# Banded attention and a gated projection on one core: two rotating pairs of score banks, a joint maximum, convolution from SBUF, and a new written order

## The chip, the cores and the metric

The kernel runs on one core of one Trainium2 chip. Its engines work from queues of their own, each in order: TensorE (PE, whose weight loads are shown apart as PEld), VectorE (DVE), ScalarE (ACT), GpSimd (POOL), and SyncE (SP), which here issues DMA transfers. PSUM, where PE writes, has eight banks of 512 float32 columns for each of 128 partitions; the DVE and ACT instructions of this kernel read it, its POOL instructions do not. The metric is the device time of one execution in microseconds (us), lower is better.

## The reference

Two stages follow one another. The first is attention with a window of 128 keys and 4 sink keys, for 4 batches, 8 heads, 768 positions and 64 columns a head:

```python
scores = scale * np.matmul(q, k.transpose(0, 1, 3, 2))
keep = is_sink | in_window          # key < 4, or 0 <= query - key < 128
scores = np.where(keep, scores, -1000000000.0)
scores = scores - np.max(scores, axis=-1, keepdims=True)
a = np.exp(scores)
a = a / (np.sum(a, axis=-1, keepdims=True) + 1e-09)
return np.matmul(a, v).astype(np.float32)
```

The second takes the heads side by side as x (768 x 512 a batch), gates a projection of x with a causal convolution of five taps, and projects again:

```python
for k in range(K):
    gate_pre += conv_w[k][None, None, :] * xp[:, k:k + S, :]
gate = 1.0 / (1.0 + np.exp(-gate_pre))
val = x @ w_val
return (gate * val @ w_out).astype(np.float32)
```

## The kernel before, in words

**Tiling.** The work is cut into 24 steps s, each a batch b, one of three blocks of 256 queries p (so p is s // 2 % 3), and one of two groups of four heads. Two steps that follow one another (the two groups of heads) make one of 12 tiles m of the second stage. In step s:

- load_kq (kq) and load_v (vv) fetch keys, queries and values; the tiles of keys and of queries have three buffers each.
- scores(s, g) for g = 0 and 1 (s0, s1) issues 32 small matmuls into the two banks ss (L364), patches the band with a predicated copy (L369), and takes in four instructions the masked, negated scores to SBUF and their extremes to ngm (L374).
- exps (e0, e1) computes four exponentials with their sums on ACT (L382). recip (rec, L387 and L388) inverts the sums on DVE. normalise (norm, L396 to L403) scales on POOL.
- probs_t (tx, ty) transposes on PE (L413), each half into one of two banks tr. probs_x (ev) masks on DVE (L435, L437), probs_y (yv) copies on ACT (L444). sinks_t and sinks_e (sk, ts) do the same for the sink columns.
- values and sinks (val, si) multiply by the values on PE into the two banks xv (L461, L468). x_copy and x_high (xc, xh) copy the result out on ACT (L478, L482); x_low (xl) makes the remainder on POOL (L492). x_head (hd) writes the last four columns of the block before in front of xv, in PSUM.
- conv_last (c4, POOL, L496) makes the last tap; conv (c0, c1, L504) adds the other four on DVE, eight instructions a step, reading x from PSUM and the running sum from SBUF. gate (th, L509) is a tanh on ACT.

For each tile m: val (v0 to v3, L523) is the first projection in four blocks of 12 matmuls, gated (g0, g1, L534) multiplies on DVE from PSUM, gated_h and gated_l (h, l; L538, L542) split into high and low parts on ACT and POOL, outp (o0 to o3, L553) is the second projection in blocks of 6 matmuls, store (t0, t1, L557) copies out and stores. Both projections, the sink transposes and the weight decoding share two banks acc. Banks: ss 2, xv 2, tr 2, acc 2.

**Start.** The weights come as 64-bit floats and are decoded on ACT, DVE, POOL and PE (load_weights, decode_weights; events l and a to f of each of four chunks of w_val and w_out) between the first steps. Matmuls of zeros (busy, L225) stand before and between the first scores.

**Order.** Nothing is planned while building: every event has a due time, its step plus a number of the tables WHEN and EARLY (or DECODE), the events are sorted by it, and each engine's queue is filled in that order:

```python
for _, f, args in sorted(events, key=lambda e: e[0]):
    f(*args)
```

Of the kernel before, what the change touches and what calls it, by code (L numbers as in the profile page):

```python
# [35 lines left out]
WHEN = dict(kq=-1.9615, vv=-0.3611, s0=-0.1928, e0=0.4814, s1=0.3255, e1=0.5848, rec=0.6245, vl=1.4302, norm=0.667,  # L36
            tx=0.9562, ty=1.2383, sk=1.1919, ev=1.1901, yv=1.3942, ts=1.226, val=1.8427, si=1.874, xc=2.044,
            xh=2.2668, hd=2.0069, xl=2.2917, c4=2.0938, c0=2.2838, c1=2.5363, th=2.774, v0=0.4208, v1=0.4433,
            v2=0.7542, g0=0.6699, v3=0.8679, h0=0.7252, l0=1.0416, g1=0.9504, h1=1.0551, l1=1.282, o0=1.3729,
            o1=1.5265, o2=1.3969, t0=2.127, o3=2.081, t1=2.5321, cw=-67.148)  # L40

EARLY = {("kq", 0): -111.3041, ("vv", 0): -51.6322, ("s0", 0): -67.4875, ("e0", 0): -63.9472, ("s1", 0): -63.8218,
# [156 lines left out]
def banded(ctx, tc, wts, cw, zero, ident, scalars, flag, qt, kt, vt, vsk, w_val, conv_w, w_out, out):  # L199
# [393 lines left out]
    for t in skb:  # L593
        nc.gpsimd.memset(t, 0.0)
# [211 lines left out]
```

## Time and profile before

| what | value |
|---|---|
| three runs | 282.65, 279.63, 282.4 us; median 282.4 |
| span of the profiled execution | 279.6 us (no time outside the span is listed) |
| PE busy | 264.6 us (95%) |
| DVE busy | 221.2 us (79%) |
| ACT busy | 181.0 us (65%) |
| POOL busy | 175.4 us (63%) |
| granted PE clock, mean | 0.987 |

A line of the groups reads: line, engine, operation, tile written <- tiles read, shape, count | busy us, mean ns of one | idle us of the engine before them, and what ended it. The chain of waits is followed back from the last instruction to whatever released each one; its pieces are shown in order of time. Busy PE time is modelled from pipelined matmuls, so it is not PE at its peak.

### The profile page before, as it was taken

To read this page: it belongs to the slowest core of one execution; us is meant where nothing else is said; L and a number is where in the kernel's file an instruction comes from. 1 tells how busy PE (TensorE), PEld (TensorE's weight loads), DVE (VectorE), ACT (ScalarE), POOL (GpSimd) and SP (SyncE) were. 2 spreads that over 40 slices of the span, in tenths; PEclk is the share of its full clock that TensorE was granted. 3 is DMA by queue.
4 is the path that set the end of the run, shared out by engine and by line. 5 is a ranking of instruction groups with operands and counts; after the bars stand their busy time and mean duration, and the time that the engine had idled before them with its cause. 6 is when DMAs were issued, how large, how long until landed. Compare 5 with 4: busy or idle time off the path is not lost.

```text
span 279.6 us, 9649 instructions
## 1 busy us (share of the span) xinstructions
PE 264.6 (95%) x3748; PEld 211.1 (75%) x3752; DVE 221.2 (79%) x827; ACT 181.0 (65%) x605; POOL 175.4 (63%) x226
## 2 busy tenths in 40 slices
PE   8897599999999999999999999999999999999991
PEld 3444358769878879789789788788788788798880
DVE  5899969997879787986977987996896898887510
ACT  3799949838757765764875784685676667564421
POOL 3378956883965874675585757648658729647330
PEclk9999989999999999999999999999999999999997
DMA  6993952028416515516417317326336241020202
GB/s 191 328 373 129 303 158 96 4 85 291 140 49 212 157 38 194 155 41 211 140 40 246 101 67 225 101 84 205 97 93 212 87 134 56 6 75 0 77 5 82
DMA packets 27396, 36.95 MB, mean 132 GB/s; under 512 B 2256, under 2 KB 23760, under 8 KB 27344
## 3 DMA queue, kind: packets, MB, share of 16 engines
q1 hardware_dynamic: 27344, 36.27, 40.4%
q8 instruction: 31, 0.51, 0.8%
q14 instruction: 21, 0.17, 0.2%
HBM read 29.97 MB, written 6.29 MB: 130 GB/s over the span
## 4 chain that ended last, share of the span: by engine, by line
PE 77%; POOL 7%; DVE 7%; ACT 5%; issue 1%; POOLq 0%; ACTq 0%
PE acc L523 23%; PE acc L553 21%; PE xv L461 11%; PE ss L364 9%; PE tr L413 5%; PE acc L225 3%; PE xv L468 3%; POOL wx L396 2%; DVE sg L504 2%; ACT w L382 2%; DVE sx L374 2%; POOL sg L496 1%; ACT xt L478 1%; POOL xl L492 1%; POOL wol L179 1%
## 5 line engine op out<-in xcount | busy, mean ns | idle before, releaser
L396 POOL TENSOR_TENSOR wx<-w,sm 128x512 f32<-128x512 f32 x48 | 49.2, 1047 | 59.9 <-DVE sm L388 53.2
L504 DVE SCALAR_TENSOR_TENSOR sg<-xv,cw,sg 128x256 f32<-128x256 f32 x192 | 78.9, 475 | 5.9 <-POOL sg L496 5.9
L382 ACT ACTIVATE w<-sx,ngm 128x132 f32<-128x132 f32 x192 | 75.1, 399 | 4.1 <-DVE ngm L374 4.1
L523 PE MATMUL acc<-xh,wvh 128*128 128x256 f32 x192 | 49.3, 291 | 0.4 <-ACT xh L482 0.4
L523 PE MATMUL acc<-xh,wvl 128*128 128x256 f32 x192 | 47.1, 279 | 0.0
L374 DVE CUSTOM_DVE_ANT_0 sx<-ss,mask 128x132 f32<-128x132 f32 x192 | 45.2, 292 | 1.6
L553 PE MATMUL acc<-woh,gh 128*128 128x512 f32 x96 | 40.0, 416 | 0.0
L364 PE MATMUL ss<-k,q 64*32 64x168 f32 x1536 | 38.5, 309 | 1.4 <-DVE ngm L374 0.8
L523 PEld LDWEIGHTS acc<-xh,wvh 128*128 128x128 f32 x192 | 36.1, 188 | 3.8 <-DVE sg L504 1.3
L553 PE MATMUL acc<-wol,gh 128*128 128x512 f32 x96 | 38.1, 397 | 0.3 <-POOL wol L179 0.3
L553 PE MATMUL acc<-woh,gl 128*128 128x512 f32 x96 | 38.1, 396 | 0.0
L382 ACT ACTIVATION_READ_ACCUMULATOR w<-sx,ngm 128x1 f32 x192 | 37.2, 194 | 0.0
L461 PEld LDWEIGHTS xv<-wt,v 64*64 64x64 f32 x1024 | 30.3, 133 | 8.1 <-issue 5.1
L523 PEld LDWEIGHTS acc<-xh,wvl 128*128 128x128 f32 x192 | 36.1, 188 | 0.0
L542 POOL TENSOR_TENSOR gl<-sg,gh 128x512 fp32r<-128x512 f32 x24 | 31.5, 1312 | 5.7 <-ACT gh L538 5.7
L461 PE MATMUL xv<-wt,v 64*64 64x192 f32 (+2 forms) x1024 | 34.5, 278 | 0.5 <-ACT wt L444 0.5
L496 POOL TENSOR_TENSOR sg<-xt,cw 128x512 f32<-128x512 f32 x24 | 25.2, 1051 | 11.4 <-ACT xt L478 11.3
L364 PEld LDWEIGHTS ss<-k,q 64*32 64x32 f32 x1536 | 22.4, 106 | 12.8 <-issue 3.6
L492 POOL TENSOR_TENSOR xl<-xt,xh 128x512 fp32r<-128x512 f32 x24 | 30.9, 1289 | 1.7 <-ACT xh L482 1.7
L523 PE MATMUL acc<-xl,wvh 128*128 128x256 f32 x192 | 30.9, 281 | 0.9 <-POOL xl L492 0.9
L413 PE MATMUL tr<-ident,wx 128*128 128x128 f32 x192 | 28.2, 274 | 0.0
L523 PEld LDWEIGHTS acc<-xl,wvh 128*128 128x128 f32 x192 | 26.0, 188 | 1.4 <-POOL xl L492 1.3
(110 smaller groups left out, 423.5 us busy)
## 6 DMA issues: line engine op xcount, KB each, us to landing
k<-in_kt_dram SPq DMA_DIRECT2D x23, 408.0 KB, 4.0
v<-in_vt_dram SPq DMA_DIRECT2D x16, 384.0 KB, 3.3
out_dram<-osb SPq DMA_DIRECT2D x24, 256.0 KB, 2.1
q<-in_qt_dram SPq DMA_DIRECT2D x23, 256.0 KB, 4.3
raw<-in_w_val_dram SPq DMA_DIRECT2D x4, 512.0 KB, 6.7
v<-in_vt_dram SPq DMA_DIRECT2D x8, 256.0 KB, 4.2
raw<-in_w_out_dram SPq DMA_DIRECT2D x4, 512.0 KB, 6.2
vs<-in_vsk_dram SPq DMA_DIRECT2D x8, 128.0 KB, 4.1
```

The lines of the kernel that those rows point to most:

```text
L364: nc.tensor.matmul(ss[e * QB:(e + 1) * QB, j, c * n + x0:c * n + x1], q[js, g, (4 * c + e) * QB:(4 * c + e + 1) * QB], k[js, g, (2 * c + e ...
L374: nc.vector.tensor_tensor_reduce(out=sx[:, j, c], in0=sv[:, j, c, :PK], in1=mask[:, c if p == 0 else 2], op0=ALU.add, op1=ALU.min, scale=- ...
L382: nc.scalar.activation(out=w[:, g, j, c], in_=sx[:, j, c], func=AF.Exp, scale=-1.0, bias=ngm[:, g, j, c:c + 1], accum_out=sm[:, g, j, c:c ...
L396: nc.gpsimd.tensor_tensor(out=t[:, n].rearrange("p c h x -> p h c x"), in0=w[:, :, :, at], in1=sm.to_broadcast([P, 4, 2, D]), op=ALU.mult)
L413: nc.tensor.transpose(out=x[:, o:o + P], identity=ident, in_=ws[s][:, n, c, 2 * g:2 * g + 2].rearrange("p j x -> p (j x)"))
L461: nc.tensor.matmul(acc[o * D:(o + 1) * D, g, x0 + h * D:x0 + (h + a1 - a0 + 1) * D], v[js, g, n], t[js, g, n, a0:a1 + 1].rearrange("p a r ...
L492: nc.gpsimd.tensor_tensor(out=xl[:, g], in0=xts[s], in1=xh[:, g].bitcast(F32), op=ALU.subtract)
L496: nc.gpsimd.tensor_tensor(out=sg[s // 2][:, g], in0=xts[s], op=ALU.mult, in1=cw[:, g, KT - 1:].to_broadcast([P, 2, PQ]))
L504: nc.vector.scalar_tensor_tensor(out=g, in0=x, scalar=a, in1=g, op0=ALU.mult, op1=ALU.add)
L523: nc.tensor.matmul(acc[:, h], a[:, kc, cs], x[:, kc], start=(n == 0), stop=(n == 11))
L542: nc.gpsimd.tensor_tensor(out=gl, in0=g, in1=gh.bitcast(F32), op=ALU.subtract)
L553: nc.tensor.matmul(acc, a[:, kc, ts], x[:, kc], start=(kc + n == 0), stop=(kc + n == 5))
```

## The change

- **Banks.** ss and tr go. Two pairs of banks take their place, handed out in turn by pair() to each scores call and each probs_t call (tx, which now does both halves), in the order of the list. Banks: pairs 4, xv 2, acc 2.
- **Maximum.** In steps with p above 0 the four instructions of L374 are replaced by one maximum over the four blocks, straight from PSUM, and a small scaling by -0.125; the exponentials then read the pair of banks in PSUM with scale 0.125. Steps with p = 0 keep the four instructions with the mask.
- **Convolution.** x_copy writes x to SBUF behind four columns for the head, x_head copies the head there too, and conv reads SBUF (six buffers xt in place of four).
- **First projections.** val_copy (y0, y1) copies a projection out to SBUF on ACT; the list has it for m = 0 and 1 only.
- **Start.** The first queries and the first chunk of w_val are fetched over ACT's queue; identity, blanks and the table load (warm_up, now near the end) become events; the index patterns of masks get a place each; the fills of zeros are other counts.
- **Order.** The tables of due times are replaced by one written list. Names are as above, with px, py for ev, yv, sv for the sink values and vl for val(s).

```diff
-    ss = ps_s.tile([P, 2, 512], F32, name="ss", tag="ss")
-    for j in range(2):
-        nc.tensor.matmul(ss[:, j], zero[:, :P], zero, start=True, stop=True)
+    pairs = [ps_s.tile([P, 2, 512], F32, name=f"pr{n}") for n in range(2)]
+    for x in pairs:
+        for j in range(2):
+            nc.tensor.matmul(x[:, j], zero[:, :P], zero, start=True, stop=True)
+
+    def pair():
+        pairs.append(pairs.pop(0))
+        return pairs[-1]
...
+            (nc.scalar if s == 0 else nc.sync).dma_start(out=q[:, hs], in_=qt[b, gs, :, p * PQ:(p + 1) * PQ].rearrange("g p x -> p g x"))
...
+        (nc.scalar if (n, c) == ("wv", 0) else nc.sync).dma_start(out=raw, in_=src)
...
     def scores(s, g):
...
         n = 2 * HB + D
+        ss = pair()
...
+        if p:
+            sxs[s, g] = sv
+            nc.vector.tensor_reduce(out=ngm[:, g], in_=sv[:, :, :, :PK], axis=mybir.AxisListType.X, op=ALU.max)
+            nc.vector.tensor_scalar(out=ngm[:, g], in0=ngm[:, g], scalar1=-0.125, scalar2=None, op0=ALU.mult)
+            return
...
     def exps(s, g):
...
-                nc.scalar.activation(out=w[:, g, j, c], in_=sx[:, j, c], func=AF.Exp, scale=-1.0,
+                nc.scalar.activation(out=w[:, g, j, c], in_=sx[:, j, c, :PK], func=AF.Exp,
+                                     scale=0.125 if steps[s][1] else -1.0,
                                      bias=ngm[:, g, j, c:c + 1], accum_out=sm[:, g, j, c:c + 1])
...
-    def probs_t(s, n):
-        trs[s, n] = x = ps_t.tile([P, 512], F32, name="tr", tag="tr")
...
+    def probs_t(s):
+        trs[s] = x = pair()
+        for n in range(2):
+            for g in range(2):
+                for c in range(2):
+                    o = (2 * g + c) * P
+                    nc.tensor.transpose(out=x[:, n, o:o + P], identity=ident,
+                                        in_=ws[s][:, n, c, 2 * g:2 * g + 2].rearrange("p j x -> p (j x)"))
...
+            xts[s] = p2.tile([P, 2, KT - 1 + PQ], F32, name="xt", tag="xt", bufs=6)
...
     def x_copy(s):
...
+        nc.scalar.activation(out=xt(s)[:, :, KT - 1:], in_=accs[s], func=AF.Copy)
...
-        nc.scalar.activation(out=accs[s][:, :, :KT - 1], func=AF.Copy,
-                             in_=xts[s - 2][:, :, PQ - KT + 1:] if steps[s][1] else none)
+        nc.scalar.activation(out=xt(s)[:, :, :KT - 1], func=AF.Copy,
+                             in_=xts[s - 2][:, :, PQ:] if steps[s][1] else none)
...
-                g, x, a = sg[s // 2][:, c], accs[s][:, h, kk:kk + PQ], cw[:, c, kk:kk + 1]
+                g, x, a = sg[s // 2][:, c], xts[s][:, h, kk:kk + PQ], cw[:, c, kk:kk + 1]
...
+    def val_copy(m, u):
+        t = p2.tile([P, 4, P, 2], I32, name="vc", tag="raw", bufs=4)
+        x = t.rearrange("p k m t -> p (k m t)")[:, :2 * PQ].bitcast(F32).rearrange("p (h r) -> p h r", h=2)
+        nc.scalar.activation(out=x, in_=vacc[m, u], func=AF.Copy)
+        vacc[m, u] = x
...
     with tc.manual_schedule():
-        for _, f, args in sorted(events, key=lambda e: e[0]):
+        for n in ORDER.split():
+            f, args = events[n]
             f(*args)
-            if (f.__name__, args) in FILL:
-                busy(FILL[f.__name__, args])
```

In the list, with all lines left out that the prediction doesn't speak of:

```diff
+ORDER = """
+fill.7 wvl.0 fill.6 fill.4 load_conv kq.0 masks wva.0 wvb.0 hd.0 conv_weights blanks s0.0 fill.6 wvc.0 wvl.2
+wva.2 kq.1 fill.5 vv.0 signs wvd.0 e0.0 wvb.2 wvc.2 s1.0 e1.0 s0.1 e0.1 rec.0 norm.0 wve.0 wvd.2 s1.1 wve.2
...
+s0.2 wvb.1 woe.0 norm.1 wof.0 sk.0 ts.0 tx.1 py.1 px.1 e0.2 wod.0 wva.3 sv.1 wvc.1 rec.2 wvb.3 fill.10 kq.3
...
+woe.3 h1.0 l1.0 tx.3 py.3 wod.3 xh.2 s1.4 e1.4 px.3 rec.4 vv.6 kq.6 s0.6 s0.5 s1.5 o0.0 wof.3 o2.0 o3.0 kq.9
...
+py.5 c4.4 c0.3 c1.3 g0.1 th.3 sk.5 ts.5 sv.6 px.5 g1.1 h0.1 s1.7 l0.1 s1.6 e1.7 h1.1 s0.7 l1.1 vv.7 xl.4 kq.8
+s1.8 e1.6 vl.5 si.5 xh.5 xc.5 o0.1 o2.1 o3.1 vv.9 t1.1 o1.1 t0.1 xl.5 c4.5 v0.2 rec.6 e1.8 norm.6 c0.4 c0.5
...
+ts.6 g1.2 px.7 vl.6 sk.7 si.6 xh.6 xc.6 xl.6 hd.8 c4.6 h1.2 l1.2 ts.7 s1.9 e1.9 kq.11 s0.9 s0.8 vl.7 si.7 xc.7
...
+v3.3 g1.3 tx.9 py.9 px.9 sk.9 ts.9 h1.3 norm.8 tx.8 py.8 px.8 th.6 g0.3 l1.3 h0.3 o0.2 sk.8 ts.8 l0.3 s0.10
+e0.10 hd.13 s1.10 e1.10 kq.12 s0.12 hd.19 s1.11 e1.11 rec.10 norm.10 s0.11 s1.12 e0.11 vl.8 vv.12 o1.2 si.8
+xh.8 xc.8 kq.13 hd.9 vl.9 si.9 o2.3 t0.2 o3.3 xc.9 e0.12 tx.10 xh.9 sk.10 ts.10 vv.10 hd.11 t1.3 e1.12 o0.3
...
+hd.10 h0.4 tx.12 px.12 l0.4 py.12 vl.11 si.11 th.9 xc.11 xh.11 g1.4 vl.12 h1.4 c0.10 vv.13 s0.13 s1.13 s0.14
...
+norm.13 v2.5 v3.5 hd.12 c1.11 e0.14 sv.13 xh.12 xl.12 th.11 g1.5 vv.14 v1.5 g0.5 sk.13 ts.13 tx.13 px.13 kq.16
+s1.14 h0.5 l0.5 py.13 h1.5 e1.14 l1.5 s1.15 vv.16 e1.15 rec.14 c4.12 s0.15 e0.15 s0.16 s1.16 rec.15 vl.13
...
+v3.6 si.14 xh.14 xc.14 c4.14 vv.15 c0.13 c1.13 xl.14 th.12 v1.6 g0.6 vl.15 th.13 g1.6 kq.19 s1.19 h0.6 vv.17
+l0.6 h1.6 e1.19 l1.6 s0.17 e0.17 s0.18 s1.17 tx.16 px.16 si.15 py.16 xc.15 o0.6 o1.6 hd.17 c4.15 c0.15 scalars
...
+h1.7 l1.7 s1.18 kq.20 e1.18 rec.18 s0.19 s0.20 e0.19 vl.17 si.17 xh.17 vv.20 xc.17 o0.7 o2.7 o3.7 c0.16 kq.23
...
+o0.8 norm.20 o1.8 o2.8 vv.22 c4.19 xl.19 c0.18 c1.18 kq.22 o3.8 t1.8 t0.8 tx.20 px.20 sk.20 th.18 py.20 s1.21
+s1.22 e1.21 xl.18 e1.22 ts.20 rec.21 s0.22 e0.22 vl.20 vv.23 v0.9 v1.9 c0.19 si.20 rec.22 xc.20 norm.21 tx.21
...
+s1.23 s0.23 e0.23 si.21 xc.21 e1.23 tx.22 o2.9 o3.9 px.22 py.22 o0.9 hd.22 o1.9 t1.9 xh.21 c0.20 c4.21 xl.21
...
+v3.11 warm_up l0.11 t0.10 g1.11 h1.11 o0.11 o2.11 l1.11 o3.11 t1.11 o1.11 t0.11
+"""
```

More of the change, by code (lines that the diff above doesn't have):

```diff
@@ L34 @@
 BIG = 1.0e30
[L36 to L40, printed above, removed]
@@ L262, in banded @@
     mk = p2.tile([P, 6, P], F32, name="mk", tag="dec_t")
-    d, d0, c4, t0, t1, ti = (mk[:, n] for n in range(6))
+    d, d0, c4, t0, t1 = (mk[:, n] for n in range(5))
     low = cn.tile([P, D], U8, name="low")
@@ L266, in banded @@
     prev = cn.tile([P, D], F32, name="prev")
-    mask = cn.tile([P, 3, PK], F32, name="mask")
+    mask = cn.tile([P, 2, PK], F32, name="mask")
     none = cn.tile([P, 2, KT - 1], F32, name="none")
@@ L306, in banded, with signs, blanks @@
     minus = cn.tile([P, P], F32R, name="minus")
-    nc.gpsimd.tensor_scalar(out=plus, in0=ident, scalar1=1.0, scalar2=None, op0=ALU.mult)
-    nc.gpsimd.tensor_scalar(out=minus, in0=ident, scalar1=-1.0, scalar2=None, op0=ALU.mult)
+    def signs():
+        make_identity(nc, ident)
+        nc.gpsimd.tensor_scalar(out=plus, in0=ident, scalar1=1.0, scalar2=None, op0=ALU.mult)
+        nc.gpsimd.tensor_scalar(out=minus, in0=ident, scalar1=-1.0, scalar2=None, op0=ALU.mult)
     skb = [cn.tile([P, P], F32, name=f"skb{n}") for n in range(2)]
+    def blanks():
+        for t in skb:
+            nc.gpsimd.memset(t, 0.0)
     raws, dec = {}, {}
@@ L406, in banded @@
     probs, trs, skt, sktp = {}, {}, {}, {}
-    def probs_t(s, n):
-        trs[s, n] = x = ps_t.tile([P, 512], F32, name="tr", tag="tr")
-        for g in range(2):
-            for c in range(2):
-                o = (2 * g + c) * P
-                nc.tensor.transpose(out=x[:, o:o + P], identity=ident,
-                                    in_=ws[s][:, n, c, 2 * g:2 * g + 2].rearrange("p j x -> p (j x)"))
+    def probs_t(s):
[6 more added lines that the diff above has]
+                                        in_=ws[s][:, n, c, 2 * g:2 * g + 2].rearrange("p j x -> p (j x)"))
     def sinks_t(s):
@@ L467, in sinks, with xt @@
         for g in range(2):
-            nc.tensor.matmul(accs[s][:, g, KT - 1:KT - 1 + PQ], vs[b, qd][:, g],
+            nc.tensor.matmul(accs[s][:, g], vs[b, qd][:, g],
                              skt[s].rearrange("p c r -> p (c r)"), start=False, stop=True, skip_group_check=True)
     xts = {}
+    def xt(s):
+        if s not in xts:
+            xts[s] = p2.tile([P, 2, KT - 1 + PQ], F32, name="xt", tag="xt", bufs=6)
+        return xts[s]
     def x_copy(s):
-        if steps[s][2] == 0:
-            xs[s // 2] = tuple(p2.tile([P, 4, PQ], F32R, name=n, tag=n) for n in ("xh", "xl"))
-            sg[s // 2] = p2.tile([P, 4, PQ], F32, name="sg", tag="sg")
@@ L477, in x_copy, with half @@
-        xts[s] = t = p2.tile([P, 2, PQ], F32, name="xt", tag="xt", bufs=4)
-        nc.scalar.activation(out=t, in_=accs[s][:, :, KT - 1:KT - 1 + PQ], func=AF.Copy)
+        nc.scalar.activation(out=xt(s)[:, :, KT - 1:], in_=accs[s], func=AF.Copy)
+    def half(d, s, n, dtype):
+        if s // 2 not in d:
+            d[s // 2] = p2.tile([P, 4, PQ], dtype, name=n, tag=n)
+        return d[s // 2][:, 2 * steps[s][2]:2 * steps[s][2] + 2]
     def x_high(s):
-        g, o = slice(2 * steps[s][2], 2 * steps[s][2] + 2), KT - 1
@@ L524, in val @@
             n += 1
+    def val_copy(m, u):
[3 more added lines that the diff above has]
+        vacc[m, u] = x
     def halves(m, u):
         us = slice(2 * u, 2 * u + 2)
+        if m not in gs:
+            gs[m] = tuple(p2.tile([P, 4, PQ], F32R, name=n, tag=n) for n in ("gh", "gl"))
         return sg[m][:, us], gs[m][0][:, us], gs[m][1][:, us]
     def gated(m, u):
[L531 to L532 removed]
         g = halves(m, u)[0]
@@ new lines, in banded @@
+    events = {f"{n}.{x}": (f, (x,) + args) for n, (f, args) in acts.items() for x in range(len(steps))}
+    for f in (masks, signs, blanks, warm_up, scalars, flag, load_conv, conv_weights):
+        events[f.__name__] = f, ()
+    for n in ("wv", "wo"):
+        for c in range(4):
+            events[f"{n}l.{c}"] = load_weights, (n, c)
+            for k in range(6):
+                events[f"{n}{'abcdef'[k]}.{c}"] = decode_weights, (n, c, k)
+    for n in range(1, 20):
+        events[f"fill.{n}"] = busy, (n,)
@@ L728, with warm_up @@
     flag_i = cp.tile([P, 1], I32, name="flag_i")
+    def warm_up():
+        nc.scalar.activation(out=warm, in_=warm, func=AF.Exp)
     def scalars():
```

131 lines of the change are left out of this document (63 added, 68 removed), and 48 rows, old and new, of tables (DECODE, EARLY).

## The prediction

> **What bounds the kernel now.** I read the busy sums by stage first, then the chain of waits in order of time, then the durations by line. The sums by stage (stretch, its length, then busy time and instructions of PE, PE's weight loads, DVE, ACT and POOL, then PE's clock and the DMA):
>
> ```profile
> 0.00:10.00 10.00, 8.59 (x75) 3.45 (x83) 6.63 (x36) 3.50 (x7) 3.85 (x15) 1.00 0.72 215
> 10.00:20.00 10.00, 8.88 (x145) 4.03 (x127) 9.01 (x38) 10.00 (x37) 5.07 (x8) 1.00 1.05 372
> 20.00:30.00 10.00, 7.79 (x94) 5.04 (x94) 9.61 (x31) 9.47 (x29) 9.09 (x13) 1.00 0.57 184
> 30.00:40.00 10.00, 7.73 (x107) 4.34 (x114) 7.71 (x26) 5.91 (x21) 7.43 (x9) 0.83 0.67 226
> 40.00:50.00 10.00, 9.23 (x156) 8.07 (x138) 9.76 (x29) 9.07 (x29) 6.28 (x8) 1.00 0.35 106
> 50.00:60.00 10.00, 9.38 (x109) 6.57 (x102) 9.86 (x36) 6.59 (x25) 8.35 (x8) 1.00 0.01 2
> ...
> 260.00:270.00 10.00, 9.52 (x66) 8.64 (x66) 4.58 (x10) 3.81 (x7) 3.97 (x4) 1.00 0.13 48
> 270.00:279.60 9.60, 3.64 (x16) 2.61 (x14) 0.00 (x0) 1.20 (x2) 0.89 (x1) 0.81 0.18 63
> sum 279.60, PE 264.64 PEld 211.11 DVE 221.24 ACT 181.04 POOL 175.41; mean PE 12.60 PEld 10.05 DVE 10.54 ACT 8.62 POOL 8.35
> ```
>
> Up to 60 us the vector engine is the full one: 6.63 + 9.01 + 9.61 + 7.71 + 9.76 + 9.86 = 52.6 us of 60, so only 7.4 us of it are idle. After that the tensor engine is the full one, as the chain shows. Its columns are start, length, engine, tile and line:
>
> ```profile
> 57.84 2.12 PE acc L553 x8
> ...
> 93.47 0.73 PE ss L364 x32
> 94.20 4.39 PE acc L553 x18
> ...
> 113.53 0.73 PE ss L364 x32
> ...
> 263.34 4.71 PE acc L523 x38
> 268.05 5.60 PE acc L553 x24
> 273.67 0.60 ACT osb L557
> ```
>
> From 93.47 to 113.53 us, one pair of steps, the chain never leaves PE: 20.1 us, with each 0.73 us score group alone between blocks of projections (the 18 at 94.20), values and transposes. So a faster VectorE, ScalarE or GpSimd gains nothing there; only the first 58 us and the tail could give time. From the first output projection at 57.84 to 273.67 PE passes 215.8 us, about 1 us of it idle (0.48 in 260 to 270). Behind it stand 5.9 us of store and DMA.
>
> **The change part by part.** *Score banks.* Today a group of scores has its own pair of banks, free again once VectorE has taken the four maxima. Now scores and transposes take two pairs strictly in turn, and in the 16 steps with p above 0 the exponentials read the pair itself, so it is held until ScalarE is through. The terms, from the timeline (start, duration, engine, line):
>
> ```profile
> 149.95 0.43 DVE L369 COPY_PREDICATED ss<-low,ss 128x256 f32<-128x256 uint8 x1 [0.55 <-PE ss L364]
> 150.41 0.29 DVE L374 CUSTOM_DVE_ANT_0 sx<-ss,mask 128x132 f32<-128x132 f32 x1
> ...
> 151.28 0.08 DVE L374 DVE_READ_ACCUMULATOR2_ANT ngm<- 128x1 f32 x1
> ...
> 155.30 0.41 ACT L382 ACTIVATE w<-sx,ngm 128x132 f32<-128x132 f32 x1
> ...
> 156.77 0.19 ACT L382 ACTIVATION_READ_ACCUMULATOR w<-sx,ngm 128x1 f32 x1
> ```
>
> VectorE's part is 149.95 to 151.36, 1.41 us. Four exponentials last from 155.30 to 156.96, 1.66 us. The single maximum over 4 x 132 values from PSUM and the small scaling are not in the trace. Near rows:
>
> ```profile
> L435 DVE TENSOR_TENSOR wt<-tr,cur 128x512 f32<-128x512 f32 x24 | 16.5, 687 | 9.2 <-PE tr L413 9.2
> L387 DVE TENSOR_SCALAR sm<-sm 128x8 f32<-128x8 f32 x24 | 4.6, 192 | 1.1 <-ACT w L382 1.1
> L478 ACT ACTIVATE xt<-xv 128x512 f32<-128x512 f32 x24 | 14.4, 598 | 9.5 <-PE xv L468 8.8
> L509 ACT ACTIVATE sg<-sg 128x512 f32<-128x512 f32 x24 | 15.0, 625 | 12.0 <-DVE sm L387 7.3 <-DVE sg L504 4.6
> ```
>
> 0.46 + 0.69 + 0.19 = 1.34 us against 1.41: no gain worth counting (bounds 0.2 us either way per group). The exponential from PSUM stays at 1.66 us; the PSUM copy L478 is 4% shorter than L509 from SBUF, and that is its lower bound. So a pair is tied up for 0.73 + 1.41 = 2.14 us with p = 0, and for 0.73 + 1.41 + 1.66 = 3.80 us otherwise, if VectorE and ScalarE are free at once.
>
> *New order.* PE takes the list in order, and the list now puts score groups behind one another with no other PE work between. Behind a waiting group stands all of PE's queue. Walked with the terms above, idle VectorE and ScalarE, and PE's first group at 0:
>
> s0.10, s1.10, s0.12, s1.11, s0.11, s1.12: the third needs the first pair back at 3.80; the fourth waits for e1.10, which ScalarE starts at 3.80, so 5.46; the fifth goes at 6.19; the sixth waits for e1.11 (scores to 6.19, maxima to 7.60, exponentials to 9.26). It ends at 9.99 us for 6 x 0.73 = 4.38 us of work: 5.6 us idle. s1.14, s1.15, s0.15, s0.16, s1.16: starts at 0, 0.73, 3.80, 5.46, 7.60, end 8.33, work 3.65: 4.7 idle. s1.23, s0.23, si.21, tx.22: the transposes need e1.23, which stands behind e0.23 and a 0.60 us copy on ScalarE: 3.55 + 1.66 + 0.60 + 1.66 = 7.47, with 1.7 us done: 5.8 idle. s1.19, s0.17, s0.18, s1.17: 3.3. s1.9, s0.9, s0.8 and s1.21, s1.22, s0.22: third start at 3.80, 2.3 each. s0.13, s1.13, s0.14 and s1.18, s0.19, s0.20 (third start at 2.14): 0.7 each.
>
> One run also waits for a transfer. The key and query tiles have three buffers; kq.8 is issued just ahead of s1.8, and until s1.6 is through all three are held (steps 6, 7 and 9).
>
> ```profile
> k<-in_kt_dram SPq DMA_DIRECT2D x23, 408.0 KB, 4.0
> ```
>
> In s1.7, s1.6, s0.7, s1.8 the last cannot start before 1.46 + 0.4 (the queries are issued behind the keys, an estimate; their landing is taken like the keys') + 4.0 = 5.9 us: work 2.9, end 6.6, idle 3.7. Stores and value loads behind it on SP wait for nothing that PE needs soon.
>
> *One accumulator pair for values.* It stays single. vl.12 follows si.11 at once and waits for the tanh (L509, 0.6) and both copies (2 x 0.60): 1.8. vl.9 behind si.8 waits 1.2. Together 3.0.
>
> Sum of idle: 5.6 + 4.7 + 5.8 + 3.3 + 4.6 + 1.4 + 3.7 + 3.0 = 32.1 us. Lower bound, with 1.21 for VectorE and 1.59 for ScalarE: the six-group run has 5.0 in place of 5.6, so 28.5 in all. Upper: work of either engine that stands ahead of a group in its queue adds to each wait; I allow a quarter, 40.
>
> *Convolution from SBUF.* Same 192 instructions, now with two SBUF inputs. No such f32 form with 256 columns is in the trace; the weight decoding has one with 512, beside the gate product, which reads PSUM:
>
> ```profile
> L504 DVE SCALAR_TENSOR_TENSOR sg<-xv,cw,sg 128x256 f32<-128x256 f32 x192 | 78.9, 475 | 5.9 <-POOL sg L496 5.9
> L534 DVE SCALAR_TENSOR_TENSOR sg<-sg,acc 128x512 f32<-128x512 f32 x24 | 16.0, 668 | 13.7 <-PE acc L523 13.5 <-ACT sg L509 0.2
> L154 DVE SCALAR_TENSOR_TENSOR wv_t<-wv_p,wv_t x4: 691/692/1416, 6.6 to 19.6; 128x512 int32<-128x512 int32 x4
> ...
> 28.54 1.22 POOL L496 TENSOR_TENSOR sg<-xt,cw 128x512 f32<-128x512 f32 x1
> 28.90 1.41 DVE L154 SCALAR_TENSOR_TENSOR wo_t<-wo_p,wo_t 128x512 int32<-128x512 int32 x1
> ```
>
> Undisturbed, 0.69 us from SBUF stands against 0.67 from PSUM, so I take no change (475 ns). Under a GpSimd instruction the same form takes 1.41, 0.72 longer: it ends 0.55 us after L496's end at 29.76. These waits fall on VectorE beside PE's projections; I count 0 in the sum and 10 us in the range, since VectorE has 279.6 - 221.2 = 58 us free, and 30 more once PE idles. [...]
>
> *The start.* Before the first output projection the new list has three more score groups and a reciprocal on VectorE (3 x 1.41 + 0.4) and one convolution call of four less (4 x 0.41, the call's 78.9 / 192): 2.9 us more. Two pairs let PE run ahead, so VectorE's 7.4 us of idle could at best go; five more warming matmuls and a later transfer (kq.6 right ahead of s0.6, 4.0 us) work against it. Bounds 57.8 - 7.4 + 2.9 = 53 and 65; I take 57.8, no change. The moved table load, identity, blanks, and the ScalarE-queue transfers lie in this stretch beside VectorE's work: nothing. The copies of the first projections (four of 0.6 us on ScalarE, idle 0.9 to 4 us of each ten there from 30 us on) free banks early: nothing.
>
> *Sum.* 57.8, plus 215.8 - 1.0 - 2.1 (three score groups already done, less a small transpose) = 212.7 of PE work, plus 32.1 idle, plus 5.9 behind PE: 308.5 us, against a span of 279.6 and the three runs of 279.6, 282.4 and 282.7. I say 308.
>
> **Rivals.** *VectorE becomes the bound.* GpSimd is busy 175.4 of 279.6 us, 63%. If each of 192 convolution instructions that meets it waits the 0.72 us of the row above, that is 192 x 0.63 x 0.72 = 87 us. 221 + 87, plus the 7 idle at the start and 15 at the end (5.4 + 9.6), is 330 us. It decides once the waits pass some 65 us, 0.34 each. For it: the 1.41 us row. Against: GpSimd's normalisation waits for VectorE's reciprocal, so the two often do not run at once. [...] Chance 0.2, time 330.
>
> *Faster: the walk does not bind.* If other PE work did fill the runs, that is, if the written list were not the order on PE, the 32 us would go and the start could give its 7.4: 279.6 - 7.4 - 2.1 = 270. It decides at gaps of under 0.3 us between s0.10 and s1.12. Against it: the chain of before follows its list group by group. Chance 0.09. *No change,* 280 to 283: half of the runs filled and half of the start gained away, 0.05.
>
> **Numbers.** The forecast has 0.66. Its own range is 300 (idle 28.5, the start at 53) to 326 (idle 40, waits 10). 290 to 328 reaches half-way to the cases where part of the runs is filled and most of the way to VectorE's; it leaves out the faster cases and the far ends, 2 in 10. A measurement of this kernel tells about 1% from no change. Faster 0.09, same 0.05, slower 0.86.
>
> **What would show it.** In the profile after: PE idle waiting for ScalarE's exponentials, some 30 us of it past 58 us, where before had 1; the waits at s0.12, s1.11 and s1.12 of 2 to 3 us each; a wait of some 4 us for keys or queries ahead of s1.8; the convolution's mean above 475 ns with a maximum near 1.5 us; the first output projection at 55 to 62 us. It is wrong if PE is still gap-free from 100 to 200 us, or if the first output projection comes before 50.

## The result, and the profile after

| | before | after |
|---|---|---|
| median of four runs | 281.9 us (279.6 to 282.7) | 387.6 us (386.4 to 389.1) |
| ratio, 95% interval | | 1.379 (1.372 to 1.387) |
| span of the profiled execution | 279.6 us | 384.6 us |
| mean granted PE clock | 0.987 | 0.888 |
| first output projection starts | 52.6 us | 71.7 us |

The direction was forecast, the size was not: 308 us forecast, 290 to 328 the range, 387.6 measured. The medians of the runs below are over the runs within 1.5% of a kernel's fastest, so e2, e9 and e10 stand 1 to 3 us under the medians over all of their runs.

The first output projection before starts at 52.6 us and not at 57.84, where the prediction put it. By 57.84, the start of a piece of the chain, 16 of its matmuls were done. Its first row (start, length, engine, line):

```profile
52.56 0.50 PE L553 MATMUL acc<-woh,gh 128*128 128x512 f32 x1
```

The sums by stage, cut at the first output projection and at the end of PE's work (columns as in the prediction's first fence), before and after:

```profile
0.00:52.50 52.50, 44.40 (x582) 26.66 (x586) 45.19 (x167) 39.86 (x126) 34.23 (x52) 0.97 0.64 210
52.50:273.70 221.20, 220.23 (x3174) 184.45 (x3166) 176.05 (x661) 140.61 (x481) 141.18 (x175) 1.00 0.36 115
```

```profile
0.00:71.80 71.80, 49.22 (x676) 30.77 (x676) 62.82 (x158) 43.68 (x140) 43.43 (x61) 0.87 0.53 169
71.80:378.20 306.40, 239.76 (x3071) 200.46 (x3071) 201.80 (x477) 135.97 (x468) 143.18 (x165) 0.90 0.25 79
378.20:384.60 6.40, 0.00 (x0) 0.00 (x0) 0.00 (x0) 0.60 (x1) 0.00 (x0) 0.68 0.25 90
```

In the second stretch PE has 103 matmuls fewer than before (96 of them are three score groups, which now come earlier) but is busy 19.5 us longer, at a granted clock of 0.90, and it is idle 306.4 - 239.8 = 66.6 us, where it was idle 1.0 before. VectorE is not full there: 201.8 of 306.4 us, two thirds. Still it carries the chain of waits, of which over the whole span 40% is VectorE and 35% PE. Its pieces in order of time (start, length, engine, tile, line), for one pair of steps:

```profile
88.03 1.60 DVE sg L520 x3
...
90.68 4.43 DVE sg L520 x9
95.11 0.60 DVE sg L556
95.71 0.60 DVE wt L446
96.31 0.61 DVE wt L448
...
97.05 0.88 PE pr L363 x32
...
98.36 3.68 DMA q<-in_qt_dram
...
102.18 1.37 PE pr L363 x32
103.55 2.77 PE xv L473 x48
```

From 88.03 to 96.92 the chain stays on VectorE, but for 1.04 us listed as issue: twelve convolution instructions (L520), and behind them in its queue the gated product (L556) and the masks of the transposes (L446, L448) for which the score group at 97.05 waits, as these empty the pair. Here the queue of VectorE, not its sum, sets PE's pace. The groups of VectorE by line (as before: busy, mean ns | idle before), after:

```profile
L520 DVE SCALAR_TENSOR_TENSOR sg<-xt,cw,sg 128x256 f32<-128x256 f32 x192 | 115.5, 668 | 6.1 <-POOL sg L512 6.1
L372 DVE TENSOR_REDUCE ngm<-pr 128x4 f32<-128x528 f32 x32 | 22.6, 707 | 1.1
```

The convolution (before 78.9 us, mean 475 ns) takes 36.6 us more.

### The profile page after: what moved, and what is told of

The parts are those of the page before. It is cut to its first block, busy times and chain, and to the rows that moved or that the text cites. A ratio compares the mean times of both kernels' runs of the same rounds, so it can differ in the third digit from the quotient of the medians.

```text
span 384.6 us, 9486 instructions
## 1 busy us (share of the span) xinstructions
PE 289.0 (75%) x3746; PEld 231.2 (60%) x3746; DVE 264.6 (69%) x635; ACT 180.2 (47%) x609; POOL 186.6 (49%) x226
## 4 chain that ended last, share of the span: by engine, by line
DVE 40%; PE 35%; ACT 10%; issue 3%; DMA 1%; POOL 1%; SPq 0%; ACTq 0%; DVEq 0%
DVE sg L520 20%; PE acc L575 14%; PE xv L473 7%; ACT w L386 6%; PE pr L363 5%; PE acc L539 5%; DVE ngm L372 3%; DVE wt L446 2%; DVE wt L448 2%; DVE pr L368 2%; DVE sg L556 2%; PE pr L419 2%; DVE ngm L373 1%; PE xv L480 1%; DVE sx L378 1%
## 5 line engine op out<-in xcount | busy, mean ns | idle before, releaser
L520 DVE SCALAR_TENSOR_TENSOR sg<-xt,cw,sg 128x256 f32<-128x256 f32 x192 | 115.5, 668 | 6.1 <-POOL sg L512 6.1
L363 PE MATMUL pr<-k,q 64*32 64x168 f32 x1536 | 43.5, 353 | 43.7 <-ACT w L386 16.6
L401 POOL TENSOR_TENSOR wx<-w,sm 128x512 f32<-128x512 f32 x48 | 52.5, 1114 | 44.0 <-DVE sm L393 31.0
L363 PEld LDWEIGHTS pr<-k,q 64*32 64x32 f32 x1536 | 26.3, 118 | 57.1 <-ACT w L386 20.9
L386 ACT ACTIVATE w<-pr,ngm 128x132 f32<-128x132 f32 x128 | 45.6, 378 | 18.1 <-DVE ngm L373 14.4
L507 POOL TENSOR_TENSOR xl<-xt,xh 128x512 fp32r<-128x512 f32 x24 | 32.1, 1339 | 35.6 <-ACT xt L491 25.5
L473 PE MATMUL xv<-wt,v 64*64 64x192 f32 (+2 forms) x1024 | 42.6, 320 | 3.9 <-ACT xh L499 1.4
L446 DVE TENSOR_TENSOR wt<-pr,cur 128x512 f32<-128x512 f32 x24 | 16.4, 683 | 38.4 <-PE pr L419 23.2
L419 PE MATMUL pr<-ident,wx 128*128 128x128 f32 x192 | 27.9, 292 | 10.1 <-ACT w L386 6.5
L455 ACT ACTIVATE wt<-pr 128x512 f32<-128x512 f32 (+1 forms) x24 | 13.5, 561 | 44.3 <-DVE wt L448 36.6
L368 DVE COPY_PREDICATED pr<-low,pr 128x256 f32<-128x256 uint8 x48 | 20.3, 423 | 18.2 <-PE pr L363 14.4
L419 PEld LDWEIGHTS pr<-ident,wx 128*128 128x128 f32 x192 | 23.8, 151 | 12.3 <-POOL sg L512 6.6
```

The source lines that it names most:

```text
L363: nc.tensor.matmul(ss[e * QB:(e + 1) * QB, j, c * n + x0:c * n + x1], q[js, g, (4 * c + e) * QB:(4 * c + e + 1) * QB], k[js, g, (2 * c + e ...
L368: nc.vector.copy_predicated(sv[:, :, :, :D], low[:, None, None, :].to_broadcast([P, 2, 2, D]), sv[:, :, :, 2 * HB:])
L386: nc.scalar.activation(out=w[:, g, j, c], in_=sx[:, j, c, :PK], func=AF.Exp, scale=0.125 if steps[s][1] else -1.0, bias=ngm[:, g, j, c:c + ...
L401: nc.gpsimd.tensor_tensor(out=t[:, n].rearrange("p c h x -> p h c x"), in0=w[:, :, :, at], in1=sm.to_broadcast([P, 4, 2, D]), op=ALU.mult)
L419: nc.tensor.transpose(out=x[:, n, o:o + P], identity=ident, in_=ws[s][:, n, c, 2 * g:2 * g + 2].rearrange("p j x -> p (j x)"))
L473: nc.tensor.matmul(acc[o * D:(o + 1) * D, g, h * D:(h + a1 - a0 + 1) * D], v[js, g, n], t[js, g, n, a0:a1 + 1].rearrange("p a r -> p (a r) ...
```

## The experiments

I set four theories against each other: the **order** (score groups written behind one another), the **convolution** (two SBUF inputs wait for GpSimd), the **hold** (a pair is tied up until the exponentials are through), and the **clock** (PE's work is longer because PE idles). All ratios are to the kernel before, run beside them on the same chip.

| run | order | convolution | maxima | us | ratio (95%) |
|---|---|---|---|---|---|
| after | new | two inputs | joint | 387.6 | 1.379 (1.372 to 1.387) |
| e3 | new | two inputs | four | 368.8 | 1.313 (1.306 to 1.319) |
| e2 | new | one input | joint | 353.0 | 1.256 (1.243 to 1.268) |
| e8 | new | one input | four | 335.6 | 1.198 (1.192 to 1.204) |
| e7 | old | two inputs | joint | 335.2 | 1.194 (1.188 to 1.200) |
| e15 | old | two inputs | four | 329.0 | 1.173 (1.164 to 1.182) |
| e13 | old | one input | four | 290.5 | 1.033 (1.025 to 1.041) |

All seven have the changed code with two pairs in turn. Where the table says one input, the multiply-add of the taps is left out. Three steps lead from e13 up to the changed kernel: the convolution 38.5 us, the joint maximum with its hold 6.2, the new order 52.4. Taken the other way, from e13 by e8 and e2, the order comes to 45.1, the hold to 17.4 and the convolution to 34.7, so a part's share depends on what else is in.

### The order

**The changed code in the old order** (e1). The old due times, written as a list under the new names; the copies y0 and y1, which its expectation counts in, are left out:

```diff
-s0.10 e0.10 ... s1.10 e1.10 ... s0.12 ... s1.11 e1.11 ... s0.11 s1.12
+(each step's groups between other PE work, as the due times of before put them)
```

> All of the changed code, with the old order of the work: both first-half and second-half banks, the joint maximum, the convolution from SBUF and the early copies stay, only the written list is that of before (the two transposes of a step, which are one call now, stand where the first of them stood). If the order is what costs (groups of scores written behind one another, VectorE's weight decoding put ahead of what PE waits for), nearly all of the 105.7 us goes: 280 to 300 us. If the convolution with two SBUF inputs is what costs, by its waits on GpSimd, the waits stay: 330 us or more, with the convolution's mean near 600 ns. If the held pairs cost by themselves, in any order, 320 us or more, with PE waiting for exponentials for over 20 us.

347.2 us, ratio 1.237 (1.230 to 1.244), the convolution's mean 633 ns: the second theory fits. The order is a part too, 40 us, but not the whole. 13 calls of exponentials stood behind the group that takes their pair again and read its scores, so I mended that:

```diff
-s0.2 ... s1.2 ... e0.2
+s0.2 ... e0.2 s1.2          (13 such steps; and y0, y1 of the first two tiles in again)
```

> The changed code in the old order once more, with the exponentials of 13 first score groups moved ahead of the second group of their step. In the run before of this order they stood behind the group that takes their pair again, so that run did not wait for them; their inputs were a later group's scores. The four copies of the first projections, left out there, are in again. The theory that the order costs some 40 us and the convolution and the pairs the rest: 345 to 360 us. If the held pair costs as much in the old order as in the new one (19 us), up to 370.

335.2 us, ratio 1.194 (1.188 to 1.200), below the expected 345: with the exponentials earlier and the copies in, 12 us went. So the order's share is 387.6 - 335.2 = 52.4 us.

**Where the order costs** (e10, e14). The list was cut at o0.0, the first output projection; what either list has ahead of that cut stays ahead of it, so e10 has four more events there, and e14 nine, three of them score groups:

```diff
-new list up to o0.0, new list behind it
+e10: new list up to o0.0, old order behind it (e0.5 moved ahead of tx.4)
+e14: old list up to o0.0, new list behind it
```

> The changed code with the new list up to the first output projection and the old order behind it (335.2 us with the old order throughout, 387.6 with the new one). The first output projection came 14.0 us later in the changed kernel than in the one before. If the cost of the order lies in the first stretch, the time is 345 to 350 us or more (335 and 10 to 15); if the start only looks late and the rest makes it up, 335 to 340 us. What then is left to 387.6, some 40 us, lies in the written runs behind the first projection.

> The changed code with the old list up to the first output projection and the new one behind it. The new front with the old rest took 331.9 us against 335.2 with the old order throughout. If the runs of score groups behind the first projection make the whole cost of the order, 380 to 392 us; if front and rest share it, 350 to 370 us.

330.7 us, ratio 1.178 (1.170 to 1.186), and 393.5 us, 1.405 (1.395 to 1.415). The new front costs nothing at the end, although e10's first output projection starts at 70.8 us against e7's 65.1. Of the later steps three more score groups are then done (13 against 10); that this is what makes up for the late start is not shown. All of the order's cost that these two runs show lies behind the cut.

### The convolution

**Alone, in the kernel before** (e4), and then with an instruction of one input (e5):

```diff
-                g, x, a = sg[s // 2][:, c], accs[s][:, h, kk:kk + PQ], cw[:, c, kk:kk + 1]
+                g, x, a = sg[s // 2][:, c], xts[s][:, h, kk:kk + PQ], cw[:, c, kk:kk + 1]
...
-                nc.vector.scalar_tensor_tensor(out=g, in0=x, scalar=a, in1=g, op0=ALU.mult, op1=ALU.add)
+e5:             nc.vector.tensor_reduce(out=g, in_=x[:, :, None], axis=mybir.AxisListType.X, op=ALU.max)
```

> The kernel before, with one part of the change: the convolution reads its input from SBUF (with the four head columns copied there), in the old order and with the old banks. By my prediction's working it costs nothing to 10 us on the path: 280 to 292 us. If the waits between VectorE and GpSimd are the main cause, the convolution's mean goes from 475 to 600 ns or more, VectorE becomes full and the time is 310 us or more.

> The kernel before with the convolution from SBUF (the run that took 313.4 us), but each of the 192 convolution instructions is the one with a single SBUF input, so the multiply-add of the taps is left out. If the second SBUF input is what costs, by waits on GpSimd, all of the 32 us go: 278 to 285 us, and no instruction of these takes over 0.45 us. If the buffers, the head copies or the longer use of the SBUF tiles cost, 300 us or more.

313.4 us, ratio 1.115 (1.110 to 1.121), and 279.7 us, 0.996 (0.994 to 0.999). My "nothing to 10" was 32, and all of it goes once a reduction of one input takes the multiply-add's place: buffers, head copies and the copy of x cost nothing. The instruction of one input is itself a little shorter than the multiply-add was from PSUM (a mean of 409 ns against 475), so its gains can hold up to 13 us of VectorE's work besides the waits; e16 below is free of that. The timeline of e4 (start, length, engine, line; x4 is four instructions behind one another) shows the wait:

```profile
158.42 1.28 POOL L496 TENSOR_TENSOR xl<-xt,xh 128x512 fp32r<-128x512 f32 x1
158.50 3.16 DVE L508 SCALAR_TENSOR_TENSOR sg<-xt,cw,sg 128x256 f32<-128x256 f32 x4 [0.19 <-POOL sg L500]
159.78 0.80 POOL L259 TENSOR_TENSOR vh<-vs,vh 32x256 fp32r<-32x256 f32 x1
...
162.90 1.67 DVE L508 SCALAR_TENSOR_TENSOR sg<-xt,cw,sg 128x256 f32<-128x256 f32 x4
```

With GpSimd at work four instructions take 3.16 us, without it 1.67. The single-instruction durations in e4 go from 433 to 1521 ns with a median of 477. In e5 they go from 368 to 422, with GpSimd busy 175.4 us as before (178.2 in e4):

```profile
L508 DVE TENSOR_REDUCE sg<-xt x192: 368/409/422, 30.3 to 262.5; 128x256 f32<-128x256 f32 x192
```

**In the changed kernel, new order** (e2: the same replacement).

> The changed kernel with each of the 192 convolution instructions replaced by a VectorE instruction of the same output that reads one SBUF input and no second (a maximum over one element), so the multiply-add of the four taps is left out. If waits between VectorE and GpSimd over two SBUF inputs are what makes VectorE the bound, the 36.6 us that the convolution took more than before go and the time falls by as much or more, to 350 us or below. If the order costs, VectorE is only idle for longer: 375 us or more.

353.0 us, 34.7 less than the changed kernel, just above the 350 of the convolution theory and far from the order theory's 375. So most of the 36.6 us that the convolution took more lie on the path, and VectorE's waits are one cause among others.

**Is it GpSimd?** (e16) In e4, most of GpSimd's work goes:

```diff
-        for n, at in enumerate((slice(0, D), slice(HB, PK))):
+        if s > 1:
+            ws[s] = ws[s - 2]
...
+        for n, at in () if s > 1 else enumerate((slice(0, D), slice(HB, PK))):
...
+        if s > 3:
+            return
...
+        if m > 1:
+            return
```

The first part is in normalise (from the third step on), the two returns are in x_low and gated_l.

> The kernel before with the convolution from SBUF (313.4 us, mean of the convolution 694 ns, GpSimd busy 178 us), from which most of GpSimd's work is left out: the normalised probabilities and the low halves of values and gates are computed for the first four steps and taken again afterwards, so the values differ. GpSimd keeps some 70 to 80 us. If the convolution waits for GpSimd, its mean falls to some 530 ns and the time to 285 to 292 us. If it waits for something else (ScalarE, transfers), the mean stays above 640 ns; a shorter time alone proves nothing, as the chain passed through GpSimd too.

280.1 us, 0.999 (0.996 to 1.002). The convolution, with two SBUF inputs as in e4, by line in e4 and then in e16:

```profile
L508 DVE SCALAR_TENSOR_TENSOR sg<-xt,cw,sg 128x256 f32<-128x256 f32 x192 | 121.5, 694 | 8.9 <-POOL sg L500 8.9
```

```profile
L515 DVE SCALAR_TENSOR_TENSOR sg<-xt,cw,sg 128x256 f32<-128x256 f32 x192 | 86.4, 514 | 3.9 <-POOL sg L507 3.8
```

GpSimd fell from 178.2 to 81.9 us busy, the mean from 694 to 514 ns. Together with e5 this shows the cause from both sides: with the reduction of one input none of the 192 takes over 422 ns beside 175.4 us of GpSimd work; with 81.9 us of it in place of 178.2 the multiply-add's mean is 180 ns lower.

### The pairs and the hold

**Two pairs in turn alone, in the kernel before** (e6), then with the joint maximum and exponentials from the pair (e11):

```diff
+        ss = pair()
...
-        trs[s, n] = x = ps_t.tile([P, 512], F32, name="tr", tag="tr")
+        if n:
+            return
+        trs[s] = x = pair()
```

e11 adds the changed kernel's branch for p above 0 in scores and its scale in exps, and where the pair comes round again:

```diff
+            if f is scores and args[1] == 1 and steps[args[0]][1]:
+                exps(args[0], 0)
```

> The kernel before with one part of the change: scores and transposes take two pairs of banks in turn, and a step's eight transposes of each half are one call of sixteen with a pair of its own. Maxima to SBUF, convolution from PSUM and the order are those of before. The changed code in the old order took 347 us and the convolution alone 313, so some 34 us are open. If the pairs taken in turn cost by themselves (a score group stands behind the transposes, and these behind VectorE's and ScalarE's copies), 295 to 315 us, with PE waiting for the copies. If they cost only together with a late VectorE, 280 to 288 us.

> The kernel before with the two pairs of banks taken in turn (291.4 us alone), and in steps with p above 0 one maximum over four blocks and exponentials straight from the pair; a step's first exponentials are issued ahead of its second score group where the pair comes round again. Convolution from PSUM, old order. If holding a pair over the exponentials costs by itself, 300 to 310 us, with PE waiting for ScalarE; if only the written runs of score groups (or a late VectorE) make it cost, 288 to 295 us.

291.4 us, ratio 1.038 (1.033 to 1.043), between the two ranges expected, and 328.3 us, 1.167 (1.160 to 1.174). (In e11 three of the calls of exponentials are issued twice, at most 3 x 1.66 = 5 us of ScalarE.) The hold costs 37 us here, where the theory had 19 at most (310 us). PE's waits in e11 (us, times, longest), and the chain:

```profile
PE pr L369 <- ACT w L392: 35.1, 17, 4.4
```

```profile
146.63 0.45 PE xv L481 x2
...
147.16 0.19 ACT xv L499
...
147.37 0.60 ACT xt L491
147.97 0.49 ACT osb L570
148.46 0.49 ACT xh L495
148.95 0.36 ACT w L392 x3
...
149.41 0.94 ACT w L392 x5
...
150.40 0.81 PE pr L369 x32
```

The exponentials stand in ScalarE's queue behind four copies, the first of which waits for PE's product at 146.63, and PE's next score group waits for the exponentials: a round trip between two queues. Here the pair is held until ScalarE's queue is through, and not for the exponentials' 1.66 us alone.

**Four maxima again, in the new order** (e3, e8) **and in the old** (e15):

```diff
-        if p:
+        if False:
...
-                    out=sx[:, j, c], in0=sv[:, j, c, :PK], in1=mask[:, c], op0=ALU.add,
+                    out=sx[:, j, c], in0=sv[:, j, c, :PK], in1=mask[:, c if p == 0 else 2], op0=ALU.add,
```

> The changed kernel, but every step takes its four masked maxima to SBUF as before, so a pair of banks is free again after VectorE's 1.4 us and not only after the exponentials. By the theory of the held pair as my prediction had it (idle of 22 us for runs of score groups with p above 0, of which some 4 would remain) the time falls by 15 to 20 us at once, and by some 30 with the tensor clock that rises with it: 350 to 370 us. If VectorE or the convolution sets the pace, the pairs are free early and nobody uses it: 380 us or more.

> The changed kernel in its own order, with both the one-input convolution (356 us alone, the multiply-add of the taps left out) and the four maxima to SBUF (369 us alone). If the two costs lie one behind the other on the path, both gains add: 337 us. If a shared one, a late VectorE, stands behind both, 345 to 356 us. What is then left over before's 281 us is the order's and the pairs' own cost: by my walk the terms that stay (keys, values, groups of p = 0 and maxima) are 12 us, which would be 295 us; by the first stretch, 14 us more.

> The changed code in the old order with the four maxima to SBUF; the convolution from SBUF is the real one. If the pairs' 10 us and the convolution's 32 us add, 323 us, and the hold costs only 12 us on top of them (335.2). If the hold's 37 us of the run without the SBUF convolution are hidden behind VectorE's lateness or the reverse, 310 to 318 us.

368.8, 335.6 and 329.0 us. In the new order the hold costs 18.8 us with the slow convolution and 17.4 without (e2 less e8), so the two gains add: 387.6 - 34.7 - 18.8 = 334.1, measured 335.6. In the old order it costs 6.2 behind the slow convolution and 37 without it (e11). That the two overlap there, PE waiting for one or the other, fits these numbers but was not tested further.

**Without convolution waits and hold, old order** (e13: e15 with e5's instruction).

> The changed code in the old order, with the one-input convolution (the taps' multiply-add left out) and the four maxima to SBUF: only the pairs in turn, the merged transposes and the small parts are left of the change. If these cost what the pairs cost alone, 288 to 293 us, and the new order by itself then costs 335.6 less that, some 45 us. If something else of the changed code costs too (buffers, copies of the first projections), 300 us or more.

290.5 us, 1.033 (1.025 to 1.041), what the pairs cost alone. No other part of the changed code shows a cost here. The order by itself is then 335.6 - 290.5 = 45 us, where by my walk 12 us were to be left of the runs. The second stretch (from the first output projection to the end of PE's work) of e13 and of e8:

```profile
53.60:283.00 229.40, 223.58 (x3170) 186.79 (x3166) 165.72 (x661) 141.15 (x482) 141.67 (x175) 0.99 0.35 111
64.50:326.20 261.70, 226.70 (x3079) 192.55 (x3071) 158.49 (x629) 138.05 (x469) 133.42 (x165) 0.95 0.29 93
```

It begins 10.9 us later in e8, and PE is idle 35.0 us in it against 5.8. PE's longest waits in e8 show some of that (the 8.8 us stand ahead of the first projection):

```profile
PE pr L363 <- DVE ngm L378: 10.2, 13, 1.0
PE pr L363 <- DVE sm L392: 8.8, 1, 8.8
PE pr L363 <- DMA q<-in_qt_dram: 5.7, 2, 3.7
```

### The clock

Products of zeros, 0.7 of the idle each, ahead of 28 waiting steps of the changed kernel (e9):

```diff
+    def warmer(n):
+        for _ in range(n):
+            nc.tensor.matmul(last[0][:, 0, PQ:], zero[:, :P], zero[:, :PQ], start=True, stop=True,
+                             skip_group_check=True)
```

> The changed kernel with small products of zeros (256 columns, written to the unused half of the value banks) put on TensorE ahead of 28 steps before which it stood idle for 1 us or more, as many as fill about 0.7 of that idle. If the lower granted clock (0.888 on average, 0.987 before) is a consequence of the idle and stretches PE's work on the path, the clock rises to 0.93 or more and the time falls by 5 to 20 us: 368 to 382 us. If the clock follows something else, or what counts is VectorE's lateness alone, it stays or rises by the added work: 386 to 400 us.

374.3 us, ratio 1.332 (1.323 to 1.341): with work added, 13 us less than the changed kernel. (The zeros go into banks whose other half holds open sums, and the result is off by a relative 0.18; all instructions of the changed kernel are there.) The clock of the changed kernel, then of e9:

```profile
core 0: 384.6 us, clock 0.888
```

```profile
core 0: 371.4 us, clock 0.958
```

So the lower clock is a consequence of PE's idle, and costs at least some 13 us of the 79 by which the forecast fell short: the fills bring the clock back only in part.

### The start alone

The kernel before with the small parts at the start (e12: index patterns at once, first weights and queries on ScalarE's queue, the table of exponentials behind them):

```diff
-            nc.sync.dma_start(out=q[:, hs], in_=...)
+            (nc.scalar if s == 0 else nc.sync).dma_start(out=q[:, hs], in_=...)
```

> The kernel before with the small parts of the change at the start alone: the four index patterns are made at once on GpSimd, the first weights and the first queries are fetched on ScalarE's queue, and the table of exponentials is loaded behind them. VectorE waits twice 0.84 us for GpSimd's patterns and 0.39 us for the first scores there. If the start's end moves with it, 1 to 2 us faster: 279.5 to 280.5 us. My prediction took it as nothing: 281 to 282 us.

280.2 us, ratio 0.997 (0.992 to 1.003): no difference that can be told. No run beat the kernel before by more than that and did the whole computation.

## Why the prediction was right or wrong

The sum was 57.8 + 212.7 + 32.1 + 5.9 = 308.5 us. Cut at 52.5, where the first output projection is in the profile before, it reads 52.5 + 218.1 + 32.1 + 5.9: the same total, with some 5 us of PE's work moved behind the cut. By these terms the profile after has 71.8 + 239.8 + 66.6 + 6.4 = 384.6, so the start is 19 us over, PE's work 22, its idle 35.

By experiments the shortfall of 79 us splits in another way. The convolution costs 35 (e2) where the sum had 0; the order without the slow convolution and the hold costs 45 (e8 less e13) where the walk had 12; the pairs taken in turn cost 10 (e6) where the sum had nothing; the hold costs 17 to 19 where the walk had some 20. The cause of the convolution's cost is shown; the 33 us more of the order and the 10 of the pairs are measured, and their causes are open in part.

**Convolution from SBUF: the step that failed.** "These waits fall on VectorE beside PE's projections; I count 0 in the sum and 10 us in the range, since VectorE has 279.6 - 221.2 = 58 us free, ...". It costs 32 us alone (e4) and 35 in the changed kernel (e2). That the undisturbed instruction is no slower was right: 432 ns at best and 478 in the median from SBUF (after), 432 and 476 from PSUM (before). That it waits for GpSimd was read rightly from one row. The error was to set 58 us of free time, a sum over the span, against waits that stand in a chain: convolution, tanh, gated product, second projection, with the maxima and the masks of the transposes queued behind it. A free stretch elsewhere doesn't pay for them. The rival had the mechanism and the wrong price and point: 87 us of waits deciding from 65 on, where 36.6 us of waits cost 35 with VectorE at 69% of the span.

**PE's work at full clock: mis-sized.** 212.7 us (218.1 by the right cut) became 239.8 at 0.90. The prediction took the durations of a PE that never idles while it forecast 32 us of idle. e9 gets 13 us back.

**The walk of the score groups: right in the total.** The idle before the named groups, from PE's timeline:

| run of groups | predicted | measured |
|---|---|---|
| s0.10 to s1.12 | 5.6 | 2.6 + 1.7 = 4.3 |
| s1.14 to s1.16 | 4.7 | 1.0 + 1.5 + 1.4 + 1.2 = 5.0 |
| s1.23 to tx.22 | 5.8 | 6.5 |
| s1.19 to s1.17 | 3.3 | 1.0 + 2.1 = 3.1 |
| s1.9, s0.9, s0.8; s1.21, s1.22, s0.22 | 2.3; 2.3 | 2.9; 3.7 + 1.4 = 5.1 |
| s0.13 to s0.14; s1.18 to s0.20 | 0.7; 0.7 | 1.0; 3.6 |
| s1.8 (its transfer) | 3.7 | 2.5 |
| values | 3.0 | 1.2 + 1.2 = 2.4 |

Six rows of that timeline (start, length, engine, line; in brackets the idle before, and what ended it):

```profile
102.18 1.37 PE L363 MATMUL pr<-k,q 64*32 64x168 f32 x32 [2.49 <-DMA q<-in_qt_dram]
...
127.75 1.25 PE L363 MATMUL pr<-k,q 64*32 64x168 f32 x32 [2.94 <-ACT w L386]
...
152.34 4.39 PE L363 MATMUL pr<-k,q 64*32 64x168 f32 x96 [2.59 <-ACT w L386]
...
186.94 0.45 PE L424 MATMUL acc<-ident,skb 128*128 128x128 f32 x1 [4.68 <-POOL sg L512]
...
267.10 0.39 PE L539 MATMUL acc<-xh,wvh 128*128 128x256 f32 x1 [3.61 <-DVE sg L556]
...
338.49 1.94 PE L419 MATMUL pr<-ident,wx 128*128 128x128 f32 x8 [6.47 <-ACT w L386]
```

Together 36.4 against 32.1, and e3 gained the 15 to 20 us that the held pair was to cost. Single rows are off: a group of s1.18 to s0.20 waits 3.61 us for late maxima, and s1.22 waits 3.66 for ScalarE's copy of the transposes that had its pair before, which the walk did not have. Most of the listed signs came too: PE waiting 23 us for ScalarE's exponentials (some 30 forecast), the wait for queries before s1.8, a mean above 475 ns with a maximum of 1.52 us. The first output projection, listed at 55 to 62 us, did not.

**What the walk left out.** 66.6 - 36.4 = 30 us of idle stand elsewhere. I walked the pairs and the value banks, not the two accumulator banks. Seven sink transposes (L424) waited 1.1 to 4.7 us each, 15.2 together, for an accumulator bank or their input, and a block of projections 3.6 us for the gated product (186.94 and 267.10 above).

That more of VectorE's lateness reaches PE by these banks is argued from the trace; no run took them alone.

**The start: wrong, and misread.** "I take 57.8, no change" (bounds 53 to 65) was 71.7, and no change would have been 52.6. PE stood 8.83 us before s0.6, while VectorE, full from 30 to 60 us, had weight decoding ahead of a maximum and of the masks:

```profile
59.18 1.63 DVE wo_t L139
...
63.04 1.78 DVE wo_p L161
64.82 0.35 DVE pr L368
...
65.20 0.72 DVE ngm L372
...
66.19 0.59 DVE wt L446
66.78 0.61 DVE wt L448
...
67.48 1.45 PE pr L363 x32
```

e10 then showed that a first projection 5.7 us later than e7's need not be lost time at the end; what the 19 us here cost is open.

**The small terms.** The joint maximum costs 0.43 + 0.71 + 0.17 = 1.31 us undisturbed, forecast 1.34. The start's small edits and the copies were rightly nothing (e12, e13). What stays open is how the 45 us of the order alone fall on single waits, and why two pairs in turn cost 10 us in the old order.

## What to carry to other kernels

When an operand moves from PSUM to SBUF, look for the instruction's waits beside GpSimd's work (here its mean went from 475 to 694 ns, e4), and price them on the chain they stand in, not against the engine's free time over the span. Holding a bank until another engine has read it ties it up until that engine's queue has come to the reading (37 us in e11), so walk the queue, and walk every bank pool that the new order touches. Where idle of PE is forecast, raise its work too: here it came back at a granted clock of 0.90.

## What the hardware showed that I had not expected

**Which VectorE instructions wait for GpSimd.** The multiply-add with two SBUF inputs waits: it takes up to 1.52 us against 0.43 at best. A reduction of the same size with one SBUF input did not (192 of them in e5, at most 422 ns). But the scaling of 128 x 4 values, one SBUF input, did: 170 ns alone, up to 1111. By line, after (least, median and longest ns of one; the second fence is the convolution before, from PSUM):

```profile
L373 DVE TENSOR_SCALAR ngm<-ngm x32: 170/170/1111, 22.0 to 334.7; 128x4 f32<-128x4 f32 x32
...
L520 DVE SCALAR_TENSOR_TENSOR sg<-xt,cw,sg x192: 432/478/1522, 35.8 to 369.2; 128x256 f32<-128x256 f32 x192
```

```profile
L504 DVE SCALAR_TENSOR_TENSOR sg<-xv,cw,sg x192: 432/476/486, 30.2 to 264.8; 128x256 f32<-128x256 f32 x192
```

The timeline after, first beside GpSimd's two products, then without:

```profile
217.27 0.71 DVE L372 TENSOR_REDUCE ngm<-pr 128x4 f32<-128x528 f32 x1
218.01 0.95 DVE L373 TENSOR_SCALAR ngm<-ngm 128x4 f32<-128x4 f32 x1
...
220.83 0.17 DVE L373 TENSOR_SCALAR ngm<-ngm 128x4 f32<-128x4 f32 x1
```

```profile
216.89 2.04 POOL L401 TENSOR_TENSOR wx<-w,sm 128x512 f32<-128x512 f32 x2 [0.50 <-PE pr L363]
```

The scaling begun at 218.01 ends at 218.96, GpSimd's two products at 218.93, with the exponentials and a held pair behind. Of the 32 scalings eight took over 170 ns (0.25 to 1.11 us), and each of the eight ends 0.03 us behind a GpSimd instruction. Why the scaling waits and the reduction doesn't, the runs don't show.

**PE's clock was lower where PE idled, and filling the idle with zeros paid.** The mean clock was 0.987 before, 0.888 after, 0.958 with the fills of e9, which made the changed kernel 13 us faster.
